# Second layer product with the activations stationary and the weights moving: tokens come out on partitions, without transposes

## The chip, the cores and the metric

The kernel runs on one core of one Trainium2 chip. The metric is the device time of one execution in microseconds (us). The time before is 2762.31 us, the median of 3 runs (2762.2 to 2765.57).

## The reference, cut to what matters

```python
def _attn_ref(x, filt_r, filt_i):              # x: 8 x 3008 x 256
    X = np.fft.rfft(x, axis=1)
    Y = X * (filt_r + 1j * filt_i)[None, :, :]
    return np.fft.irfft(Y, n=x.shape[1], axis=1).astype(np.float32)

def _moe_ref(x, w_in, w_out):                  # x: 24064 x 256, d_ff 2048
    h = x @ w_in
    g = np.where(h > 0.0, h, np.exp(np.minimum(h, 0.0)) - 1.0)
    return (g @ w_out).astype(np.float32)
```

The result of the first is the x of the second. All of it is fp32. The change concerns `g @ w_out` and what lies between it and the output in memory.

## The kernel before

Each of the 8 batches is cut into 6 tiles of 512 tokens (448 in tile m = 0), and d_ff into 4 quarters q. One (b, m, q) is called an item here; there are 192. Both layer products use a scheme with seven products of half-size blocks in place of eight, so in each item the first product has seven steps ("ups") and the second has seven ("downs"). The ups of item i are interleaved with the downs of item i-1, and other units (the transforms, the loads) are put between them at two places of the item. In `nc.tensor.matmul(out, s, v)`, s is called the stationary operand (the profile shows a weight load of it, PEld, with each matmul) and v the moving one. PSUM is the memory into which matmuls write and add up. The ups write to four rotating PSUM banks (`psM`, tile names pha to phd), from which VectorE and ScalarE make g; the downs accumulate over the four quarters in four further banks (`psO`, po).

```python
    def down_steps(b, m, q):
        ...
        def step(n):
            i, u = PLACE[n]
            for a in range(2):
                nc.tensor.matmul(po[i][:, u, 0:h], w_out[q][:, COMBO[n], a, :], g[n][:, a, :],
                                 start=..., stop=True, skip_group_check=True)
            if q == 3 and n in (5, 7):
                ...                                   # ScalarE copies the bank to k[i]
                if n == 7:
                    p3 = t[:, 0, 0:h]
                    nc.vector.tensor_tensor(out=p3, in0=p3, in1=k[0][:, 1, 0:h], op=ALU.add)
        def tail():                                   # after the last quarter
            ...
            add(c12, po[2][:, 1, 0:h], p1)            # six additions on VectorE
            add(c11, po[2][:, 0, 0:h], p1)
            add(p7, p7, c12)
            add(c12, c12, p35)
            add(c21, po[3][:, 0, 0:h], p7)
            add(c22, p7, p5)

    def o_unit(b, m):                                 # one item later
        for a in range(2):
            ...
            for u in range(2):
                for dh in range(2):
                    nc.tensor.transpose(ps[0:w, u, ts(dh, P)], c[dh][:, ds((2 * a + u) * P, w)], eye)
            nc.scalar.activation(out=o[:, 0:full, :], in_=ps[:, 0:full, :], func=AXT.Copy)
            ...                                       # stores to memory

        # the main loop, cut: U is a step of the first product, D one of the second
            for k in "UDUDUDUUD": ...
            for fn, a in plan.get((i, 0), ()): fn(*a) # o_unit, n_unit and a_unit go here
            for k in "UDUDD": ...
            up_tail(); down_tail()
            for fn, a in plan.get((i, 1), ()): fn(*a)
```

In the first product, `s5` runs the product phc and then lets VectorE add it up (`add("t4", mm(5, "c", True), g["t2"])`), and `s3` accumulates more into the same bank (`mm(3, "c", False)`), so it has to wait until that addition has read the bank. The transposes of `o_unit` stood just before `s3`.

## Time and profile before

| | before |
|---|---|
| median | 2762.31 us |
| TensorE busy | 2661.4 us, 96% |
| weight loads busy | 2281.0 us, 83% |
| VectorE busy | 2021.7 us, 73% |
| ScalarE busy | 1331.3 us, 48% |
| transposes (L424), TensorE | 50.2 us |
| copies after them (L425, L427), ScalarE | 52.4 us |

TensorE is the bound. The prediction shows the lines that carry this, and how prices per instruction are read from distances between starts.

### The profile page before, as it was taken

How to read it: one execution, taken by the hardware profiler on the slowest of the kernel's cores; microseconds unless marked ns; L12 is line 12 of the kernel's file. 1: busy time of each engine (PE TensorE's matmuls, PEld its weight loads, DVE VectorE, ACT ScalarE, POOL GpSimd, SP SyncE). 2: the span in 40 equal slices, each digit the busy share in tenths (PEclk: the TensorE clock that was granted, in tenths of full speed). 3: DMA queues.
4: the chain of work that ended last, by engine and by line, in shares of the span. 5: the costliest groups of instructions: out<-in, count | busy, mean ns of one | idle time of the engine just before them, and what ended most of it. 6: DMA issues, size and time to landing. Idle time of an engine off the chain costs nothing.

```text
span 2761.7 us, 36465 instructions
## 1 busy us (share of the span) xinstructions
PE 2661.4 (96%) x13376; PEld 2281.0 (83%) x13376; DVE 2021.7 (73%) x3428; ACT 1331.3 (48%) x2281; POOL 268.4 (10%) x322
## 2 busy tenths in 40 slices
PE   2689999999999999999999999999999999999998
PEld 1288778987899878998789877898789987899887
DVE  4777877777776777767776787767877677777776
ACT  2254455544455444554455544454454544454544
POOL 3311210002000120001200021000210012000000
PEclk7599999999999999999999999999999999999999
DMA  9654421433114331242313332143321223110100
GB/s 227 174 136 119 106 56 30 115 90 99 43 47 117 76 91 37 70 115 71 79 50 87 87 88 68 37 106 94 97 61 39 72 69 94 37 39 19 25 22 16
DMA packets 141634, 214.51 MB, mean 78 GB/s; under 512 B 25268, under 2 KB 99142, under 8 KB 141456
## 3 DMA queue, kind: packets, MB, share of 16 engines
q1 hardware_dynamic: 122656, 173.60, 24.7%
q0 software_dynamic: 17792, 36.93, 5.4%
q8 instruction: 106, 1.74, 0.3%
q10 hardware_dynamic: 1008, 1.64, 0.2%
q14 instruction: 72, 0.59, 0.1%
HBM read 137.04 MB, written 78.12 MB: 78 GB/s over the span
## 4 chain that ended last, share of the span: by engine, by line
PE 86%; DVE 7%; ACT 3%; DMA 2%; issue 2%; POOL 0%; SPq 0%; DVEq 0%; ACTq 0%; POOLq 0%
PE po L385 37%; PE pha L312 11%; PE phc L312 11%; PE phd L312 11%; PE phb L312 5%; PE psa L167 3%; PE psn L266 2%; PE pva L211 2%; PE psr L211 2%; PE pso L424 2%; DVE g L317 1%; ACT e L323 1%; ACT e L324 1%; DVE c L403 1%; DVE g L328 1%
## 5 line engine op out<-in xcount | busy, mean ns | idle before, releaser
L385 PE MATMUL po<-g,wo 128*128 128x256 f32 (+1 forms) x5376 | 1324.2, 375 | 0.0
L385 PEld LDWEIGHTS po<-g,wo 128*128 128x128 f32 x5376 | 1021.5, 190 | 116.2
L323 ACT ACTIVATE e<-g 128x512 f32<-128x512 f32 (+1 forms) x576 | 357.6, 621 | 599.5 <-DVE g L317 599.3
L324 ACT ACTIVATE e<-e 128x512 f32<-128x512 f32 (+1 forms) x768 | 477.6, 622 | 24.4
L312 PE MATMUL pha<-y,wi 128*128 128x256 f32 (+1 forms) x1536 | 396.3, 380 | 8.7 <-ACT g L332 8.6
L317 DVE TENSOR_TENSOR g<-phc,g 128x512 f32<-128x512 f32 (+1 forms) x384 | 259.5, 676 | 194.9 <-PE phc L312 194.8
L328 DVE SCALAR_TENSOR_TENSOR g<-e,g 128x512 f32<-128x512 f32 (+1 forms) x576 | 387.4, 673 | 11.6 <-ACT e L324 11.1
L323 ACT ACTIVATE e<-pha 128x512 f32<-128x512 f32 (+1 forms) x192 | 113.0, 588 | 531.1 <-PE pha L312 531.1
L312 PEld LDWEIGHTS pha<-y,wi 128*128 128x128 f32 x1536 | 285.2, 190 | 93.1 <-ACT t L238 34.1
L317 DVE TENSOR_TENSOR g<-phd,g 128x512 f32<-128x512 f32 (+1 forms) x384 | 261.0, 680 | 87.0 <-PE phd L312 66.0
L328 DVE SCALAR_TENSOR_TENSOR g<-e,pha 128x512 f32<-128x512 f32 (+1 forms) x192 | 129.4, 674 | 257.8 <-ACT e L324 257.8
L227 POOL TENSOR_TENSOR sr<-sr,sp 128x512 f32<-128x512 f32 x64 | 81.1, 1268 | 1304.4 <-DVE sp L225 1304.4
L312 PE MATMUL phc<-ys,wi 128*128 128x256 f32 (+1 forms) x768 | 195.5, 377 | 2.6 <-DVE si L224 2.6
L312 PE MATMUL phd<-y,wi 128*128 128x256 f32 (+1 forms) x768 | 195.4, 377 | 1.3
L312 PE MATMUL phb<-ys,wi 128*128 128x256 f32 (+1 forms) x768 | 193.8, 375 | 0.4 <-DVE ys L290 0.4
L312 PE MATMUL phc<-y,wi 128*128 128x256 f32 (+1 forms) x768 | 194.0, 375 | 0.0
L312 PE MATMUL phd<-ys,wi 128*128 128x256 f32 (+1 forms) x768 | 193.7, 375 | 0.0
L312 PEld LDWEIGHTS phc<-ys,wi 128*128 128x128 f32 x768 | 145.3, 191 | 23.7 <-issue 7.8
L312 PEld LDWEIGHTS phd<-y,wi 128*128 128x128 f32 x768 | 145.3, 191 | 22.5 <-PE phc L312 6.5
L332 ACT ACTIVATE g<-pha 128x512 f32<-128x512 f32 (+1 forms) x192 | 112.7, 587 | 105.3 <-PE pha L312 105.1
L312 PEld LDWEIGHTS phb<-ys,wi 128*128 128x128 f32 x768 | 145.8, 190 | 17.2 <-PE pha L312 0.7
L312 PEld LDWEIGHTS phd<-ys,wi 128*128 128x128 f32 x768 | 145.8, 190 | 16.5
(98 smaller groups left out, 2781.1 us busy)
## 6 DMA issues: line engine op xcount, KB each, us to landing
z<-t SPq DMA_DIRECT2D x192, 128.0 KB, 3.8
t<-z SPq DMA_DIRECT2D x128, 192.0 KB, 3.7
yd<-t SPq DMA_DIRECT2D x128, 192.0 KB, 2.8
t<-yd SPq DMA_DIRECT2D x192, 128.0 KB, 4.1
xc<-in_x_dram SPq DMA_DIRECT2D x88, 256.0 KB, 4.6
out_dram<-o SPq DMA_DIRECT2D x176, 128.0 KB, 2.4
f<-fd POOLq DMA_DIRECT2D x112, 192.0 KB, 3.6
tn<-tn_t SPq DMA_DIRECT2D x48, 256.0 KB, 4.2
```

What stands on the lines that cost most here:

```text
L167: nc.tensor.matmul(ps[:, u, :], w[:, r + u, :], xt[:, r + u, :], start=True, stop=True)
L211: nc.tensor.matmul(ps[:, u:u + w, :], table[k, v, :], rhs[k, u:u + w, :], start=True, stop=True)
L227: nc.gpsimd.tensor_tensor(out=sr, in0=sr, in1=p, op=ALU.subtract)
L266: nc.tensor.matmul(ps[:, ts(q, P)], t[:, i - 4 * m, ds(dh * P, P)], w[:, i - 4 * m, :], start=True, stop=True)
L312: nc.tensor.matmul(banks[key][:, a, 0:h], w_in[q][:, COMBO[n], a, :], y[n], start=start and a == 0, stop=True, skip_group_check=True)
L317: nc.vector.tensor_tensor(out=g[o], in0=i0, in1=i1, op=ALU.add)
L323: nc.scalar.activation(out=e, in_=src, func=AXT.Relu, scale=-1.0)
L324: nc.scalar.activation(out=e, in_=e, func=AXT.Exp, scale=-1.0)
L328: nc.vector.scalar_tensor_tensor(out=g[n], in0=es[n], scalar=1.0, in1=src, op0=ALU.subtract, op1=ALU.max)
L332: nc.scalar.activation(out=g["t1"], in_=mm(1, "a", True), func=AXT.Copy)
L385: nc.tensor.matmul(po[i][:, u, 0:h], w_out[q][:, COMBO[n], a, :], g[n][:, a, :], start=q == 0 and a == 0 and n in (1, 3, 6, 4), stop=True, ...
L424: nc.tensor.transpose(ps[0:w, u, ts(dh, P)], c[dh][:, ds((2 * a + u) * P, w)], eye)
```

## The change

Its intent: in the second product the weights were the stationary operand and the activations moved, so the output had model dimensions on partitions and had to be transposed before the store. With the activations stationary, the output has tokens on partitions and goes straight to memory; the transposes, their PSUM buffers and the copies behind them fall away. The diff, cut to its core:

```diff
             for a in range(2):
-                nc.tensor.matmul(po[i][:, u, 0:h], w_out[q][:, COMBO[n], a, :], g[n][:, a, :],
-                                 start=q == 0 and a == 0 and n in (1, 3, 6, 4), stop=True, skip_group_check=True)
+                for v, t in enumerate((0, h - P)):
+                    nc.tensor.matmul(po[i][:, u, v, :], g[n][:, a, t:t + P], w_out[q][:, COMBO[n], a, :],
+                                     start=q == 0 and a == 0 and v == 0 and n in (1, 3, 6, 4), stop=True,
+                                     skip_group_check=True)
             if q == 3 and n in (5, 7):
...
-                if n == 7:
-                    p3 = t[:, 0, 0:h]
-                    nc.vector.tensor_tensor(out=p3, in0=p3, in1=k[0][:, 1, 0:h], op=ALU.add)
...
+            add(c12, po[2][:, 1], p1)
+            add(c11, po[2][:, 0], p1)
             add(p7, p7, c12)
-            add(c12, c12, p35)
-            add(c21, po[3][:, 0, 0:h], p7)
+            add(p3, p3, p5)
+            add(c12, c12, p3)
+            add(c21, po[3][:, 0], p7)
             add(c22, p7, p5)
-            cs_[b, m] = c
+            o_store(b, m, o)
...
-    def o_unit(b, m):          # transposes, copies, stores: removed
+    def o_store(b, m, o):      # stores alone
...
-                at(t + PER + 4 * m + 5, 0, o_unit, b, m)
```

For m = 0, h is 224, so the two windows of 128 tokens start at 0 and 96 and overlap.

More of the change, by code (lines that the diff above doesn't have):

```diff
@@ L110 @@
     ]
-    id_d = nc.inline_tensor(np.eye(P, dtype=np.float32), name="id_t").ap()
     def pool(name, bufs, **kw):
@@ L133 @@
     gb, gr, gi = (glob.tile([P, 2, 64], FP32, name=n) for n in ("gb", "gr", "gi"))
-    eye = glob.tile([P, P], FP32, name="eye")
     w_in, w_out = ([glob.tile([P, 7, 2, P], FP32, name="%s%d" % (n, i)) for i in range(4)] for n in ("wi", "wo"))
@@ L140 @@
     fd = fdp.tile([NG, 2, 48, 2, 2, D], FP32, name="fd")
-    xs, tas, tns, t1s, t2s, ss, t3s, t4s, zs, yds, ys, g_of, po_of, cs_ = ({} for _ in range(14))
+    xs, tas, tns, t1s, t2s, ss, t3s, t4s, zs, yds, ys, g_of, po_of = ({} for _ in range(13))
     def raw(src, row, ap):
@@ L376, in down_steps @@
         if q == 0:
-            po_of[b, m] = [psO.tile([P, 2, 256], FP32, tag="po%d" % i, name="po%d" % i) for i in range(4)]
+            po_of[b, m] = [psO.tile([P, 2, 2, P], FP32, tag="po%d" % i, name="po%d" % i) for i in range(4)]
         po = po_of[b, m]
@@ L383, in step @@
             for a in range(2):
-                nc.tensor.matmul(po[i][:, u, 0:h], w_out[q][:, COMBO[n], a, :], g[n][:, a, :],
-                                 start=q == 0 and a == 0 and n in (1, 3, 6, 4), stop=True, skip_group_check=True)
+                for v, t in enumerate((0, h - P)):
+                    nc.tensor.matmul(po[i][:, u, v, :], g[n][:, a, t:t + P], w_out[q][:, COMBO[n], a, :],
+                                     start=q == 0 and a == 0 and v == 0 and n in (1, 3, 6, 4), stop=True,
+                                     skip_group_check=True)
             if q == 3 and n in (5, 7):
-                t = k[i] = kp.tile([P, 2, 256], FP32, tag="k%d" % i, name="k%d" % i)
-                nc.scalar.activation(out=t[:, :, 0:h], in_=po[i][:, :, 0:h], func=AXT.Copy)
-                if n == 7:
-                    p3 = t[:, 0, 0:h]
-                    nc.vector.tensor_tensor(out=p3, in0=p3, in1=k[0][:, 1, 0:h], op=ALU.add)
+                t = k[i] = kp.tile([P, 2, 2, P], FP32, tag="k%d" % i, name="k%d" % i)
+                nc.scalar.activation(out=t, in_=po[i], func=AXT.Copy)
         def tail():
@@ L396, in tail @@
                 return
-            p1, p5 = (k[0][:, u, 0:h] for u in range(2))
-            p35, p7 = (k[1][:, u, 0:h] for u in range(2))
-            c = [kp.tile([P, 512], FP32, tag="c%d" % i, name="c%d" % i) for i in range(2)]
-            (c11, c12), (c21, c22) = ((t[:, 0:h], t[:, h:2 * h]) for t in c)
+            p1, p5, p3, p7 = (k[i][:, u] for i in range(2) for u in range(2))
+            o = [op.tile([P, 2, D], FP32, tag="o%d" % i, name="o%d" % i) for i in range(2)]
+            (c11, c21), (c12, c22) = ((t[:, :, 0:P], t[:, :, P:D]) for t in o)
@@ L402, in add @@
             def add(o, i0, i1):
                 nc.vector.tensor_tensor(out=o, in0=i0, in1=i1, op=ALU.add)
-            add(c12, po[2][:, 1, 0:h], p1)
-            add(c11, po[2][:, 0, 0:h], p1)
+            add(c12, po[2][:, 1], p1)
+            add(c11, po[2][:, 0], p1)
             add(p7, p7, c12)
-            add(c12, c12, p35)
-            add(c21, po[3][:, 0, 0:h], p7)
+            add(p3, p3, p5)
+            add(c12, c12, p3)
+            add(c21, po[3][:, 0], p7)
             add(c22, p7, p5)
-            cs_[b, m] = c
+            o_store(b, m, o)
@@ L413, in down_steps @@
         return [(lambda n=n: step(n)) for n in DOWNS], tail
-    def o_unit(b, m):
-        c = cs_.pop((b, m))
-        for a in range(2):
-            ps = psM.tile([P, 2, D], FP32, tag="mx", name="pso")
-            o = op.tile([P, 2, D], FP32, tag="o%d" % a, name="o%d" % a)
-            full = 1 if m == 0 and a == 1 else 2
-            for u in range(2):
-                w = P if u < full else 64
-                for dh in range(2):
-                    nc.tensor.transpose(ps[0:w, u, ts(dh, P)], c[dh][:, ds((2 * a + u) * P, w)], eye)
-            nc.scalar.activation(out=o[:, 0:full, :], in_=ps[:, 0:full, :], func=AXT.Copy)
-            if full == 1:
-                nc.scalar.activation(out=o[0:64, 1, :], in_=ps[0:64, 1, :], func=AXT.Copy)
-            i0, i1 = order(m)[2 * a:2 * a + 2]
-            for f in range(2):
-                r = o[f * 64:f * 64 + 64]
-                for u, w in ((0, 2),) if i1 == i0 + 1 else ((0, 1), (1, 1)):
-                    i = (i0, i1)[u]
-                    if f and i == 0:
-                        continue
-                    n1 = N1 - i if f else i
-                    nc.sync.dma_start(raw(out, b * N + n1, [[N1 * D, 64], [-D if f else D, w], [1, D]]), r[:, u:u + w, :])
@@ new lines, in o_store, with put @@
+    def o_store(b, m, o):
+        def put(n1, n2, n, w, src):
+            nc.sync.dma_start(raw(out, b * N + n1 + N1 * n2, [[N1 * D, n], [-D if n1 > H else D, w], [1, D]]), src)
+        if m == 0:
+            (o0, o1) = o
+            put(1, 0, 64, 1, o0[0:64, 0:1, :])
+            put(46, 0, 64, 1, o0[64:128, 0:1, :])
+            put(2, 0, 64, 1, o0[32:96, 1:2, :])
+            put(45, 0, 32, 1, o0[96:128, 1:2, :])
+            put(45, 32, 32, 1, o1[0:32, 0:1, :])
+            put(3, 0, 64, 1, o1[32:96, 0:1, :])
+            put(44, 0, 32, 1, o1[96:128, 0:1, :])
+            put(44, 32, 32, 1, o1[32:64, 1:2, :])
+            put(0, 0, 64, 1, o1[64:128, 1:2, :])
+        else:
+            for a, t in enumerate(o):
+                i = 4 * m + 2 * a
+                put(i, 0, 64, 2, t[0:64])
+                put(N1 - i, 0, 64, 2, t[64:128])
@@ L556 @@
         w_fetch(14)
-        nc.scalar.dma_start(eye, id_d)
         n_unit(0, 0)
```

## The prediction

> **What bounds the kernel now.** I read the page first, its busy shares and the row of slices:
>
> ```profile
> PE 2661.4 (96%) x13376; PEld 2281.0 (83%) x13376; DVE 2021.7 (73%) x3428; ACT 1331.3 (48%) x2281; POOL 268.4 (10%) x322
> ...
> PE   2689999999999999999999999999999999999998
> ```
>
> TensorE is at nine tenths or more in every slice after the start-up, and VectorE and ScalarE have room. Busy alone does not prove that TensorE never waits, so next I read the costliest groups (line, operation, names, shapes, count, busy us, mean ns of one, idle time before them):
>
> ```profile
> L385 PE MATMUL po<-g,wo 128*128 128x256 f32 (+1 forms) x5376 | 1324.2, 375 | 0.0
> L385 PEld LDWEIGHTS po<-g,wo 128*128 128x128 f32 x5376 | 1021.5, 190 | 116.2
> ...
> L266 PE MATMUL psn<-tn,t 128*128 128x128 f32 x768 | 95.3, 278 | 11.4 <-DMA t<-yd 11.4
> ...
> L424 PE MATMUL pso<-eye,c 128*128 128x128 f32 (+1 forms) x384 | 50.2, 273 | 2.0 <-DVE g L317 1.2 <-DVE c L403 0.7
> ```
>
> L385 is the second product, the line that the change rewrites. It sat idle for 0.0 us before its matmuls: it never waits for its activations, it only takes TensorE's time. L424 is the transposes that the change removes, and they waited for 2.0 us in all. In the stretch from 170 to 2750 us TensorE was busy 2573.3 of 2580.0 us, so each us of TensorE work added or removed should be a us of the kernel's time.
>
> The mean ns of one is of no use for this: 375 ns for 256 columns and 278 ns for 128 columns are latencies of overlapped instructions. What counts is the distance from start to start. The chain of waits that ended last, asked for 1130 to 1215 us, gives it (start us, us until the next piece, engine, tile, line, count):
>
> ```profile
> 1154.96 1.51 PE po L385 x8
> 1156.47 1.78 PE psn L266 x16
> ...
> 1203.74 0.87 PE pso L424 x8
> ...
> 1207.20 1.73 PE po L385 x8
> 1208.93 1.78 PE psn L266 x16
> ```
>
> Here the price list of the case can be read. 256 moving columns cost 1.73/8 = 216 ns an instruction; 224 columns (tiles of m = 0) cost 1.51/8 = 189 ns; 128 columns with a true fp32 weight load before each cost 1.78/16 = 111.3 ns; 128 columns of a transpose cost 0.87/8 = 109 ns. The instruction that the change creates (128 fp32 columns moving, a new 128-column fp32 stationary operand each time) has the form of psn, not that of pso: the weight loads of psn take 195 ns in the mean in the groups, those of the transposes 140 ns. So I take 111.5 ns for it, which I choose a little above 111.3, because the inner steps of the psn stretch lie 111.7 ns apart and only the first is 109.
>
> The counts are per hardware instruction: each matmul in the source shows twice. 8 batches x 6 tiles x 4 quarters x 7 products x 2 halves of the contraction = 2688 matmuls, and the row has 5376.
>
> **What the Trainium skill says.** "FP8 and Floating Point Precision", section "TensorE Precision Notes", gives true fp32 as four passes through the array. The trace agrees: two instructions a matmul, and 216 ns for 256 columns is two passes each. "TensorE: Matmul & The Clock Gate", section "Back-to-back issue gap", puts the gap of a warm matmul at N/2.4 + 2.5 ns; for two passes that is 2 x 256/2.4 + 2.5 = 215.8, 189.2 for 224 and 109.2 for 128, and the trace has 216, 189 and 109 (in the transposes). The same section says that in pairs of weight load and matmul both set the spacing; psn at 111.3 against pso at 109 is such a case, by a small amount. The same page, section "LDWEIGHTS (loading the stationary operand)", puts a load at columns/1.2 ns, 107 ns for 128, so behind a 128-column fp32 matmul it should just fit; the trace shows psn sustaining 111.3 ns with a load each. So halving the moving width doesn't expose a weight load: fp32 passes leave it time.
>
> **The change, part by part.**
>
> (1) Second product. A step (one of the seven products of a quarter) is now 8 instructions of 128 columns where it was 4 of 256. Full tiles: 4 x 215.8 = 863 ns before, 8 x 111.5 = 892 ns after, +29 ns. There are 8 x 5 x 4 x 7 = 1120 such steps: +32.5 us.
>
> (2) The short tiles. For m = 0 the tile holds 2 x 224 tokens and the moving operand was 224 wide; now tokens are stationary in windows of 128 at 0 and 96, which overlap in 32 tokens, so 256 tokens are paid for. 4 x 189.2 = 757 ns becomes 892 ns, +135 ns, on 8 x 4 x 7 = 224 steps: +30.2 us. So nearly half of the cost of the change lies in a sixth of its tiles.
>
> (3) Transposes removed. 48 groups of 8, 0.87 us each: -41.8 us, and the 2.0 us of waits before them: together -43.8 us. They lie in TensorE's in-order stream, so all of it counts.
>
> (4) ScalarE loses the 96 + 8 copies of L425 and L427 (49.5 + 2.9 us), gains a little in the k copies (16 of 448 elements become 512). VectorE keeps seven half-width additions a tile (the addition p3 + p5 moves from the middle to the end); for m = 0 they get 256 elements instead of 224. Neither is the bound, so this is worth 0.
>
> (5) Stores come straight from the sums; by the code 9 transfers instead of 5 for a tile of m = 0 and 4 for the others as before, so 8 x (9 + 20) = 232 issues instead of 200. After the start-up the transfer engines are four tenths busy at most in the page's slices, so this is worth 0. At the very end the chain of additions, transposes, copies and stores loses its middle: the last addition began at 2754.42 us and the first store at 2755.76; without the transposes it could begin at about 2755.0. I put -1 us.
>
> (6) Order and waits. The changed program gives TensorE the same sequence of steps with the same waits on VectorE at the same steps; only the operands swap roles. In the trace of before the weight load of each L385 step begins at least 0.8 us after VectorE has finished the g that it uses (5th percentile 2.6 us), so making g the stationary operand, fetched one instruction early, doesn't add a wait.
>
> Sum: +32.5 + 30.2 - 43.8 - 1 = +17.9 us; 2762.3 + 17.9 = 2780 us, 0.65% slower.
>
> **Rivals.**
>
> Weight loads wholly hidden: if the spacing were 109.2 instead of 111.5 ns, 10752 x 2.3 = 25 us less, 2755 us. For it: the transposes run so. Against: psn, the same form, does not, in any stretch that I looked at.
>
> TensorE's instruction supply: 10752 pairs replace 5376, in stretches of 8 to 16 pairs; the pairs of an item (one quarter of one tile) rise from 56 to 84 in about 28 x 0.216 + 56 x 0.1115 = 12.3 us, 146 ns a pair in the mean. The Trainium skill's page "TensorE: Matmul & The Clock Gate", section "Part 2: What happens when you issue a matmul", has about 62 ns a matmul where the sequencer decodes in microcode; for a pair I would estimate 124 ns from it. Against: psn sustains 111.3 for 16 pairs, though a queue could carry that; and 124 is still under 146. If all L385 pairs took 124 ns it would cost 10752 x 12.5 = 134 us: 2914 us. The longest dense run of before (64 pairs) is 160 ns a pair in the mean, so the trace doesn't exclude it.
>
> A gain by relief: with the transposes' two PSUM buffers a tile and ScalarE's 52 us gone, other waits could shrink. For it: some matmuls of the first product wait (weight loads of pha for ACT t L238, 34.1 us in all, mostly hidden). Against: all excess gaps in TensorE's steady state outside the transform units sum to some 25 us, most of them in start-up and unit switches that stay. At best -5 us, 2775.
>
> Second-order loss: stores now wait in the sync queue for VectorE's sums, and a queue in order delays the reads behind them; the reads have two items (24 us) of lead, so I give this up to +5 us.
>
> **Range and chances.** The counts are exact and the spacing is measured on the same form; the open term is 1 ns of spacing = 10.8 us. From 110.4 to 112.8 ns that gives 2768 to 2794, which I take as the range. The band of 2% is 2707 to 2818, and only instruction supply, or an unseen stall, leaves it upward: same 0.93, slower 0.06, faster 0.01.
>
> **What would show it.** L385 with 10752 matmuls, pieces of 8 in the chain at 0.89 us and of 16 at 1.78 us, the same for m = 0; no rows for L424 and L425; TensorE still at 9 in every slice and the weight loads' busy share above 90%; idle before L385 under 3 us. It is wrong if the spacing of L385 is at 109 or above 115 ns, if "issue" appears before L385, or if VectorE's g is what its weight loads wait for.

## The result, and the profile after

The changed kernel took 2794.03 us (median of 4 runs, 2793.49 to 2795.29) against 2763.66 us of the kernel before (the three runs above and a fourth): the ratio is 1.011, with a 95% interval of 1.0093 to 1.0128. A ratio is the mean time of one kernel's fast runs over that of the other's of the same rounds, so it is not quite the ratio of the medians quoted. The direction and the band were forecast; the size was not. 30.4 us more were measured (31.8 us between the two profiled spans) where 17.9 were worked out, and the time lies just outside the range.

First the busy shares and the costliest groups of the changed kernel (columns as in the prediction):

```profile
PE 2687.6 (96%) x18368; PEld 2437.9 (87%) x18368; DVE 2022.9 (72%) x3428; ACT 1288.9 (46%) x2177; POOL 268.4 (10%) x322
...
L385 PEld LDWEIGHTS po<-wo,g 128*128 128x128 f32 x10752 | 1382.2, 192 | 49.8
L385 PE MATMUL po<-wo,g 128*128 128x128 f32 x10752 | 1386.7, 275 | 0.0
```

TensorE has 4992 instructions more: 5376 by the second product, less the 384 transposes. L385 still shows no idle time before its matmuls, so the second product itself does not wait. The chain of waits of the changed kernel, in the stretch from 1130 to 1290 us, gives the new price:

```profile
1137.79 0.89 PE po L385 x8
...
1168.75 1.78 PE po L385 x16
1170.53 1.79 PE psn L264 x16
```

Eight instructions take 0.89 us, sixteen 1.78 us. Over the whole trace, 9606 distances from one L385 start to the next within its line have a mean of 111.5 ns (111.4 without the 14 of 213 ns in the start-up). That price was right.

So something else must have grown. The busy sum can't show it; the waits can. What TensorE waited for, in the changed kernel (us in total, times, longest):

```profile
PE phc L310 <- DVE g L315: 5.0, 11, 2.5
PE phc L310 <- DVE si L222: 4.0, 14, 0.3
```

and in the kernel before there is only this for phc:

```profile
PE phc L312 <- DVE si L224: 2.6, 14, 0.2
```

The first line is new. These idle times are short because the record of an earlier matmul, 275 to 375 ns long where starts are 111 to 216 ns apart, still runs over part of the wait. Better is the distance from start to start less the price of the instruction (the prediction's estimate 2 x columns/2.4 + 2.5 ns, which its 216, 189 and 109 ns from the trace bear out), which I summed over both traces. From 240 us on, in gaps of more than 30 ns, TensorE lost 12.2 us in 31 places before phc, against 4.9 us in 14 places before; and 2.8 us against 1.0 us in the restarts right behind them (some 0.1 us more for the second instruction after a wait).

All 31 places are in items that follow a tile's end: 17 before the second phc (step `s3`) and 14 before the first (`s5`), with transform units between the tile's end and it. From 240 us on there are 46 such items; why the other 15 show no wait was not followed up.

One of the new places, in order of time (start us, length us, engine, line, operation, names, count). The kernel before, in the item after a tile ends:

```profile
1915.82 1.03 PE L312 MATMUL phc<-ys,wi 128*128 128x256 f32 x4
...
1916.48 0.42 DVE L403 TENSOR_TENSOR c<-k,k 128x256 f32<-128x256 f32 x1
...
1917.55 1.03 PE L385 MATMUL po<-g,wo 128*128 128x256 f32 x4
1918.01 0.68 DVE L317 TENSOR_TENSOR g<-phc,g 128x512 f32<-128x512 f32 x1
...
1918.41 1.04 PE L424 MATMUL pso<-eye,c 128*128 128x128 f32 x8
...
1919.29 1.03 PE L312 MATMUL phc<-y,wi 128*128 128x256 f32 x4
```

and the same item of the changed kernel:

```profile
1940.01 0.42 DVE L400 TENSOR_TENSOR k<-k,k 128x256 f32<-128x256 f32 x1
...
1940.38 1.03 PE L310 MATMUL phc<-ys,wi 128*128 128x256 f32 x4
...
1941.14 0.42 DVE L400 TENSOR_TENSOR o<-k,k 128x256 f32<-128x256 f32 x1
...
1942.11 1.05 PE L385 MATMUL po<-wo,g 128*128 128x128 f32 x8
1942.67 0.69 DVE L315 TENSOR_TENSOR g<-phc,g 128x512 f32<-128x512 f32 x1
1943.41 0.73 PEld L310 LDWEIGHTS phc<-y,wi 128*128 128x128 f32 x4 [0.43 <-DVE g L315]
```

Before, VectorE began its last addition of the tile's tail 0.66 us after the first phc (1916.48 against 1915.82), read phc until 1918.69, and TensorE, which had the transposes to do from 1918.41 to 1919.29, did not notice. Had the transposes been gone at that moment, phc would have been due at 1918.41, and VectorE would not have been done. Afterwards the tail is later by the addition that was moved into it (k<-k,k): its last addition begins 0.76 us after phc, the reading of phc ends at 1943.36, and phc, due at 1942.11 + 0.89 = 1943.00, starts at 1943.41. VectorE takes its work in order: this first phc was complete, by its record, at 1941.41, and its reading began at 1942.67, behind the tail and two more instructions.

### The profile page after: what moved, and what is told of

Read it like the earlier page. It is cut to its first block, busy times and chain, and to the rows that moved or that the text cites. A ratio compares the mean times of both kernels' runs of the same rounds, so it can differ in the third digit from the quotient of the medians.

```text
span 2793.5 us, 46413 instructions
## 1 busy us (share of the span) xinstructions
PE 2687.6 (96%) x18368; PEld 2437.9 (87%) x18368; DVE 2022.9 (72%) x3428; ACT 1288.9 (46%) x2177; POOL 268.4 (10%) x322
## 4 chain that ended last, share of the span: by engine, by line
PE 75%; DVE 13%; ACT 6%; issue 3%; DMA 2%; POOL 0%; DVEq 0%; SPq 0%; ACTq 0%; POOLq 0%
PE po L385 34%; PE pha L310 10%; PE phc L310 9%; PE phd L310 9%; PE phb L310 5%; DVE g L315 3%; PE psa L165 3%; ACT e L322 2%; ACT e L321 2%; DVE o L400 2%; PE pva L209 2%; DVE g L326 2%; PE psr L209 2%; PE psn L264 1%; DVE g L359 1%
## 5 line engine op out<-in xcount | busy, mean ns | idle before, releaser
L385 PEld LDWEIGHTS po<-wo,g 128*128 128x128 f32 x10752 | 1382.2, 192 | 49.8
L385 PE MATMUL po<-wo,g 128*128 128x128 f32 x10752 | 1386.7, 275 | 0.0
L315 DVE TENSOR_TENSOR g<-phc,g 128x512 f32<-128x512 f32 (+1 forms) x384 | 259.8, 677 | 208.6 <-PE phc L310 208.6
L326 DVE SCALAR_TENSOR_TENSOR g<-e,g 128x512 f32<-128x512 f32 (+1 forms) x576 | 387.4, 673 | 12.7 <-ACT e L322 12.7
L310 PEld LDWEIGHTS pha<-y,wi 128*128 128x128 f32 x1536 | 263.0, 191 | 78.8 <-ACT t L236 34.1
L315 DVE TENSOR_TENSOR g<-phd,g 128x512 f32<-128x512 f32 (+1 forms) x384 | 261.3, 681 | 86.9 <-PE phd L310 64.6
L310 PEld LDWEIGHTS phc<-y,wi 128*128 128x128 f32 x768 | 134.3, 191 | 19.3 <-DVE g L315 8.9
L310 PEld LDWEIGHTS phc<-ys,wi 128*128 128x128 f32 x768 | 131.5, 191 | 14.6 <-issue 6.3
L315 DVE TENSOR_TENSOR g<-phb,g 128x512 f32<-128x512 f32 (+1 forms) x192 | 129.5, 674 | 19.2 <-PE phb L310 18.6
```

The lines of the kernel that those rows point to most:

```text
L310: nc.tensor.matmul(banks[key][:, a, 0:h], w_in[q][:, COMBO[n], a, :], y[n], start=start and a == 0, stop=True, skip_group_check=True)
L315: nc.vector.tensor_tensor(out=g[o], in0=i0, in1=i1, op=ALU.add)
L326: nc.vector.scalar_tensor_tensor(out=g[n], in0=es[n], scalar=1.0, in1=src, op0=ALU.subtract, op1=ALU.max)
L385: nc.tensor.matmul(po[i][:, u, v, :], g[n][:, a, t:t + P], w_out[q][:, COMBO[n], a, :], start=q == 0 and a == 0 and v == 0 and n in (1, 3, ...
```

## The experiments

The theory, T: the missing us are waits of TensorE for VectorE in the item after a tile ends, because the tail of additions is longer by one and because the transposes filled just this time. Rivals: only the transposes matter (R1); or the price of L385 is what was wrong (R2).

**e1: the moved addition put back.**

```diff
                 nc.scalar.activation(out=t, in_=po[i], func=AXT.Copy)
+                if n == 7:
+                    nc.vector.tensor_tensor(out=t[:, 0], in0=t[:, 0], in1=k[0][:, 1], op=ALU.add)
...
-            add(p3, p3, p5)
```

> The addition p3 + p5 goes back to where it was before the change (right after the seventh product's step, not in the tail); nothing else. Theory T (the unpredicted 12 to 14 us are waits of TensorE for VectorE in the item after a tile ends, because VectorE's tail of sums is longer by one addition and the transposes no longer fill that time): 17 waits of 0.22 to 0.42 us (0.10 us more each in restart) before the first product's phc vanish or nearly, 14 waits of 0.455 us after the transform units return towards 0.35: about -9 us, 2785 us. Rival R1 (only the missing transposes matter, not the addition): 2791 us or more. Rival R2 (the spacing of L385 is what was under-predicted): unchanged, 2794 us.

Measured: 2784.14 us (5 runs, 2783.22 to 2785.38), correct; ratio to the kernel before 1.0076 (1.0064 to 1.0089). That is 9.9 us less than the changed kernel, with the work of every engine unchanged. By the sums from starts, the waits before phc from 240 us on fell from 12.2 to 2.6 us (26 places, none over 0.13 us). Of the 11 waits for the addition L315, one in start-up is left:

```profile
PE phc L310 <- DVE g L315: 2.2, 1, 2.2
```

R2 falls; R1 alone falls too: the price of L385 is still 111.5 ns, and the time is 7 us under what R1 gave.

**e2: eight transposes put back as a filler.** They transpose weights, and nobody reads the result.

```diff
+    def filler(b, m):
+        for a in range(2):
+            ps = psM.tile([P, 2, D], FP32, tag="mx", name="pso")
+            for u in range(2):
+                for dh in range(2):
+                    nc.tensor.transpose(ps[:, u, ts(dh, P)], w_in[0][:, 0, dh, :], eye)
...
+                at(t + PER + 4 * m + 5, 0, filler, b, m)
```

> The changed kernel with eight transposes of weights, which nobody reads, put back for each tile at the place of the old ones. Theory T: 48 x 0.87 = 41.8 us are added, but the 17 waits before phc, 8 us with their restarts, disappear behind them: +34 us, 2828 us, with no such waits left in the trace. Rival (the prediction's step 3: transposes are pure cost in an in-order stream): +41.8 us, 2836 us.

Measured: 2826.85 us (4 runs, 2826.29 to 2827.36), correct; ratio 1.023 (1.0216 to 1.0244). The fillers cost 32.8 us and not 41.8. In TensorE's waits of this run, the line for phc on the addition g is gone, and that for the transform units stays:

```profile
PE phc L312 <- DVE si L224: 4.1, 14, 0.3
```

By the sums from starts, 14 places before phc with 6.4 us are left: the 17 others, 7.6 us with restarts, are gone, and the rest is no more than the start-up moves from run to run. So at this place 9 us of transposes cost nothing: without them TensorE waits.

**e3: the kernel before without its transposes and copies** (wrong result; for m = 0 GpSimd zeroes the columns that the stores read beyond the sums).

```diff
-            ps = psM.tile([P, 2, D], FP32, tag="mx", name="pso")
-            o = op.tile([P, 2, D], FP32, tag="o%d" % a, name="o%d" % a)
...                                     # transposes and copies cut
+            o = c[a].rearrange("p (u d) -> p u d", u=2)
```

> The kernel before with its transposes and the copies after them taken out; the stores take the untransposed sums, so the result is wrong on purpose. The prediction's step 3: -43.8 us, 2720 us. Theory T with both causes: the tail has six additions at its end instead of seven, so the waits that appear are short, 17 x at most 0.2 us: 2720 to 2724 us. Rival R1 (the missing transposes alone make the waits, 17 x 0.4 to 0.5 us): 2728 us.

Measured: 2732.36 us (4 runs, 2730.39 to 2733.26); ratio 0.9889 (0.9874 to 0.9904), against 2762.93 us of before. The transposes were worth 30.6 us and not 43.8. My own figure for T was a miss here; the rival's is nearer. New waits appear without the added VectorE work too: from 240 us on 34 places before phc with 11.0 us and 3.1 us of restarts, 8.2 us more than before, and 2.5 us at one place in the start-up. That is 10.7 us, just what is missing between the two profiled spans (33.1 us less where 43.8 was said); the medians lie 2.5 us closer together.

```profile
PE phc L312 <- DVE g L317: 5.3, 14, 2.4
```

The two causes don't add up simply. In e1, which has the same order of additions and no transposes either, these waits are small. What differs is the length of TensorE's steps: 892 ns in e1 and 863 ns here, which gives VectorE more time per item. That this difference is the reason is argued, not shown here; e8 supports it.

**e8: 96 stationary columns instead of 128** (wrong result: 96 of the 128 tokens of a window, the other rows zero).

```diff
-                    nc.tensor.matmul(po[i][:, u, v, :], g[n][:, a, t:t + P], w_out[q][:, COMBO[n], a, :],
+                    nc.tensor.matmul(po[i][0:96, u, v, :], g[n][:, a, t:t + 96], w_out[q][:, COMBO[n], a, :],
```

> The changed kernel with only 96 of each window's 128 tokens as the stationary operand (wrong result on purpose: the other rows are zero); moving width stays 128. If the weight load sets the 111.7 ns between inner L385 instructions, the spacing falls to that of the moving stream, 109.2 ns as in the transposes: 10752 x 2.3 = 25 us less, about 2769 us. If the moving stream itself costs 111.7 ns, the time stays at 2794 us.

Measured: 2774.27 us (4 runs, 2773.89 to 2778.94); ratio 1.0044 (1.003 to 1.0058), 19.8 us less than the changed kernel. The loads are shorter, and the pieces of the chain too:

```profile
L385 PEld LDWEIGHTS po<-wo,g 128*96 128x96 f32 x10752 | 1298.9, 163 | 80.6
...
1131.52 0.87 PE po L385 x8
```

0.87/8 is 109 ns: the weight load of 128 columns is what makes 111.7 of 109.2 ns. (Fewer columns also mean fewer rows of output, which this run doesn't keep apart; but the transposes write 128 rows, with loads of 140 ns in the mean, and run at 109 ns.) The 1344 steps are 1344 x (891 - 873.5) ns = 23.5 us cheaper in all, where 891 is 109.2 + 7 x 111.7; about 4 of these come back as waits before phc, which grew from 12.2 to 16.4 us. Shorter steps on TensorE give VectorE less time, as e3 suggested.

**e4: only the tiles of m = 0 on the old path.** The old `down_steps` and `o_unit` are kept beside the new ones.

```diff
-            downs, down_tail = down_steps(*items[i - 1]) ...
+                downs, down_tail = (down_steps if items[i - 1][1] else down_steps_0)(*items[i - 1])
...
+                if m == 0:
+                    at(t + PER + 5, 0, o_unit, b, m)
```

> The changed kernel, but tiles of m = 0 take the old path (weights stationary, 224 columns moving, transposes). If the short tiles cost what step 2 says: 224 steps x 135 ns = 30.2 us less, 8 groups of transposes x 0.87 = 7.0 us more, so about -23 us: 2771 us, with some of the waits after those eight tiles filled, down to 2768. Rival: the overlap of the windows costs less than said because waits take its place: over 2776 us.

Measured: 2770.89 us (5 runs, 2770.09 to 2771.52), correct; ratio 1.0026 (1.0014 to 1.0039). That is 23.1 us less than the changed kernel, as worked out from the prediction's step 2. The waits before phc stay (12.1 us in 31 places), so this saving is the short tiles' alone.

**e5: three of the seven additions on GpSimd.**

```diff
+                if n == 7:
+                    nc.gpsimd.tensor_tensor(out=t[:, 0], in0=t[:, 0], in1=k[0][:, 1], op=ALU.add)
...
-            add(p3, p3, p5)
-            add(c12, c12, p3)
+            nc.gpsimd.tensor_tensor(out=c12, in0=c12, in1=p3, op=ALU.add)
             add(c21, po[3][:, 0], p7)
-            add(c22, p7, p5)
+            nc.gpsimd.tensor_tensor(out=c22, in0=p7, in1=p5, op=ALU.add)
```

> The changed kernel with three of the seven additions of a tile (those that read no PSUM) moved from VectorE to GpSimd. Theory T (waits for VectorE's tail): VectorE is 1.0 us earlier after each tile, the 17 waits before phc go (8 us), and the 14 after transform units, 0.455 us and its followers of 0.41 us, go as well (12 us): -18 us, 2776 us. Rival: the tail is not the only cause, and only the 10 us of the one moved addition return: 2784 us. Rival: GpSimd slows VectorE down: over 2784 us.

Measured: 2774.93 us (5 runs, 2773.52 to 2775.51), correct; ratio 1.0041 (1.0028 to 1.0053), 19.1 us less than the changed kernel. For phc, one wait in start-up is left:

```profile
PE phc L310 <- DVE g L315: 1.6, 1, 1.6
```

The 14 waits after the transform units, which the kernel before has too, went with them, and so did the wait of phd behind them. By the sums from starts, 12.2 + 2.8 us went before phc and 3.6 + 0.3 before phd, 18.9 of the 19.1 us.

**e6: the same three additions on GpSimd in the kernel before.**

```diff
-                    nc.vector.tensor_tensor(out=p3, in0=p3, in1=k[0][:, 1, 0:h], op=ALU.add)
+                    nc.gpsimd.tensor_tensor(out=p3, in0=p3, in1=k[0][:, 1, 0:h], op=ALU.add)
...                                     # and likewise c12 + p35 and p7 + p5
```

> The kernel before with the same three additions on GpSimd. Theory T: its 14 waits after transform units (0.35 us before phc, 0.41 us behind it) are the same queue on VectorE and vanish: -10 us, 2753 us. Rival: they come from VectorE's work in the transform units alone, and nothing changes: 2763 us.

Measured: 2764.5 us (5 runs, 2763.41 to 2765.94), correct; ratio 1.0006 (0.9992 to 1.0019): nothing gained, a miss of T's figure. The trace shows two things. The waits before phc are gone, 4.9 us and 1.0 us of restarts, but the wait of phd behind them stays (3.2 of 3.6 us). And there is a new wait of 6 us in start-up, where GpSimd has loads of the filter in its queue, the additions stand behind them, and the transposes need the sums. From its timeline:

```profile
214.79 0.54 POOL L508 DMA_DIRECT2D fd<-in_filt_i_dram  x1
...
217.23 0.52 POOL L511 DMA_DIRECT2D fd<-in_filt_i_dram  x1 [1.34 <-DMA fd<-in_filt_i_dram]
...
218.54 0.65 POOL L408 TENSOR_TENSOR c<-c,k 128x224 f32<-128x224 f32 x1
...
219.24 0.18 PEld L424 LDWEIGHTS pso<-eye,c 128*128 128x128 f32 x1 [6.40 <-POOL c L408]
```

**e7: the hybrid of e4 with the additions of e5 and e6.**

> Tiles of m = 0 on the old path, the others on the new one, and the three additions on GpSimd in both. By the prices: on full tiles the change costs 1120 x 28.8 = 32.3 us and saves 40 x 0.87 = 34.8 us, so without waits it is about even with the same edit of the kernel before: 2750 to 2756 us.

Measured: 2761.67 us (5 runs, 2760.46 to 2762.8), correct; ratio 0.9994 (0.9981 to 1.0006). It has the same wait in start-up, since its first tile takes the old path.

**e9 and e10: as e7 and e6, but the first tile's additions stay on VectorE.**

```diff
-            nc.gpsimd.tensor_tensor(out=c12, ...)
+            (nc.gpsimd if b or m else nc.vector).tensor_tensor(out=c12, ...)
```

> The hybrid with the three additions on GpSimd, except in the very first tile, where GpSimd still has a queue of loads of the filter in front of them and TensorE's transposes waited for it (6.4 us in the kernel before with that edit). If that wait is what ate the gain: 6 to 7 us less than without the exception (2761.7), 2755 us, faster than the kernel before by 0.3%. If not: 2761 us.

> The kernel before with the three additions on GpSimd except in the first tile. If the start-up wait is what hid the 6 us of steady waits that went: 2764.5 - 6.4, 2758 us. If GpSimd's additions cost TensorE something else in the steady state: 2763 us or more. Against the hybrid with the same edit: by prices 32.3 - 34.8 us on full tiles, so it should be slower by some 2 to 3 us, and the change on full tiles alone then pays a little.

Measured: e9 2752.7 us (5 runs, 2750.94 to 2754.17), correct, ratio 0.9962 (0.9949 to 0.9976); e10 2758.4 us (5 runs, 2757.43 to 2760.2), correct, ratio 0.9983 (0.997 to 0.9995). Both gain what the wait in start-up had taken: 9.0 us of e7 and 6.1 us of e6. e9 beats both kernels, by 11 and by 41 us. Its second product is now split: 8960 instructions of the new form and 896 of the old.

```profile
L454 PE MATMUL po<-wo,g 128*128 128x128 f32 x8960 | 1154.4, 275 | 0.0
...
L386 PE MATMUL po<-g,wo 128*128 128x224 f32 x896 | 201.7, 354 | 0.0
```

With VectorE out of the way, the change on full tiles alone is worth 5.7 us (e10 against e9), more than the 2 to 3 us that the prices give. The traces show where most of the rest is: before phd, behind the transform units, TensorE still loses 4.2 us in e10 (with restarts) and 0.8 us in e9. Against the kernel before, e9's gain of 0.4% is clear of the noise, but small.

## Why the prediction was right or wrong

- **What bounds the kernel** was right: the second product shows 0.0 us of idle time before and after. But the step from there, "each us of TensorE work added or removed should be a us of the kernel's time", rests on busy time, in which the overlapping records hide short waits; step 3 took it over.
- **Step 1, second product,** was right. The price of 111.5 ns was measured as 111.5 (the 215.8, 189.2 and 109.2 of the prediction are estimates by the formula that it cites; the trace's 216, 189 and 109 bear them out), and the reason for choosing psn over the transposes as the model, the fp32 weight load, is confirmed by e8.
- **Step 2, short tiles,** was right: e4 gives 23.1 us where 30.2 - 7.0 was said.
- **Step 3, transposes removed,** failed. The prediction put it: "They lie in TensorE's in-order stream, so all of it counts." e3 shows 30.6 us for 43.8, and e2 shows 32.8 for 41.8. In the items after a tile's end they filled the time in which VectorE was still working on the tail of sums and phc had not been read. The two lines that would have told it stood in the trace of before: phc read until 1918.69, transposes from 1918.41.
- **Step 4, VectorE's additions "worth 0",** failed. Moving p3 + p5 to the end put it in front of the addition that TensorE waits for next. e1 gives 9.9 us for this one addition in 48 tiles. VectorE is 72% busy in the mean, but takes its work in order and is late after a tile.
- **Step 5, stores and the end,** is too small to tell: from the start of the last matmul of the second product to the end it was 8.7 us before and 6.9 us after. That is 1.8 us less, where the prediction had 1 here and 0.7 among the waits of step 3.
- **Step 6, order and waits,** was right for the second product and incomplete as a whole. I looked at the slack of g for L385, which was ample (at least 0.8 us), and not at the slack of the PSUM banks that VectorE frees for the first product, which was the one that gave way.
- A small term was left out: the first 256-column instruction after a run of 128-column ones takes 218 instead of 216 ns; the changed trace has 876 of such gaps and the one before 78. With the same 2.5 ns after 224 columns (161 against 15) this is some 2.4 us more.

The gap of 13.9 us between the spans (31.8 - 17.9) is made up, by the distances from start to start, of the 17 waits before the second phc (7.6 us with restarts), 1.5 us longer waits at the 14 places after transform units (0.455 for 0.348 us), the 2.4 us of the last point, and about 2 us in start-up. The first three are taken from the steady part and firm; the start-up also moves by 1 to 2 us from run to run, so its share isn't, and some 0.4 us stay open.

Of the rivals, wholly hidden weight loads and a limit of instruction supply did not come true. "A gain by relief" had the sign wrong: what fell away was not a load on VectorE but its cover. The "second-order loss" doesn't show: TensorE's waits for transfers are 28.8, 24.1 and 11.4 us before and 27.9, 24.1 and 12.7 us after (psa, psr, psn).

Of the signs named in advance, one missed: the weight loads are busy for 87%, not above 90%. None of those that were to prove the prediction wrong appeared, since all of them watch L385, and the wait stood before phc.

## What to carry to other kernels

Work on the engine that bounds the kernel is not always worth its length: look, at each place from which it is removed, at what the next instruction waits for and when that was ready, with the removed piece taken out. An engine at 73% that takes its work in order can be late at one place of a period, and moving one addition of 0.42 us there cost 9.9 us over 48 tiles, though this engine isn't the bound. Price matmuls by the distance between starts of the nearest form in the trace, weight load included; this part held to the nanosecond.

## What the Trainium skill lacked or had wrong

- "TensorE: Matmul & The Clock Gate", section "Back-to-back issue gap", has no figure for fp32 pairs of weight load and matmul. Here 128 columns with a 128-column fp32 load each run at 111.7 ns, and with a 96-column load at 109 ns; an estimate by the page's formula for an isolated matmul, taken for two passes, is 109.2.
- The same page, section "Part 4: PE-mode transpose", gives about 275 ns for a transpose in a kernel's context. The rows here (fp32) show 273 ns as the duration of one, but in a row they cost 109 ns each; the page says that access latency makes most of its figure, but has no price for transposes in a row.
- No page that I read says that a matmul that waited is followed by a longer gap: here the second gap after a wait is longer by some 0.1 us (0.104 us at the waits for the addition, 0.075 us after the transform units).
- No page that I read says that removing work from the bounding engine can lay a wait bare: here 9 of 41.8 us (e2) and 13 of 43.8 us (e3).
